# Three zero stores of fifteen rows issued from GpSimd in the last head group, and small stores at the end

## The chip, the cores and the metric

The kernel runs on one core of one Trainium2 chip. The metric is the device time of one execution in microseconds; smaller is better. Several executions of a kernel are timed, and the median is told. Beside the times there is a profile of one execution: for each engine what it ran and when, and for the DMA engines every packet that they moved.

The names used: TensorE (PE) multiplies matrices, VectorE (DVE) and ScalarE (ACT) work on rows of data, GpSimd (POOL) runs general operations and may issue transfers, SyncE (SP) issues transfers. Transfers between the device memory (DRAM) and the on-chip memory are carried out by 16 DMA engines that all issuers share.

## The reference: what is computed

The program is one decode step of a transformer block with its gradients. The block adds an attention over the last `W = 1024` of 4096 cached keys and a gated feed-forward network to its input. Outputs are the block's result and the gradients of its input, of both caches and of all weights.

```python
def _fwd_reference(A_x, A_k_cache, A_v_cache, A_wq, A_wo, B_x, B_w_gate, B_w_up, B_w_down):
    def _A_ref(x, k_cache, v_cache, wq, wo):
        ...
        W = min(4096, max(256, Sk // 4))
        k = jnp.repeat(k_cache[:, :, Sk - W:, :], rep, axis=1)
        v = jnp.repeat(v_cache[:, :, Sk - W:, :], rep, axis=1)
        scores = jnp.einsum("bhqd,bhkd->bhqk", q, k) * (Dh ** -0.5)
        p = _softmax(scores, axis=-1)
        ...
    def _B_ref(x, w_gate, w_up, w_down):
        return (_gelu(x @ w_gate) * (x @ w_up)) @ w_down
    x = A_x
    xn = _layernorm(x, axis=-1)
    return x + _A_ref(xn, A_k_cache, A_v_cache, A_wq, A_wo) + _B_ref(xn, B_w_gate, B_w_up, B_w_down)

def reference(...):
    _out, _vjp = jax.vjp(_f, A_x, A_k_cache, A_v_cache, A_wq, A_wo, B_w_gate, B_w_up, B_w_down)
    _grads = _vjp(grad_out)
    return (jnp.asarray(_out), *[jnp.asarray(_g) for _g in _grads])
```

The caches are `(4, 8, 4096, 128)` in bfloat16: 4 batches, 8 groups of heads, 4096 keys of 128 numbers. Their gradients have the same shape, and the first `K0 = 3072` keys of each of the 4 x 8 planes of each cache took no part in the attention. Their gradient is zero, but it has to be written: 64 planes (two caches) of 3072 keys x 128 numbers x 2 bytes = 768 KB each, 48 MB in all. That is the zero filling that the change is about.

## The kernel before: the parts concerned

Zeros lie in one on-chip tile of 128 rows x 6144 numbers (12288 bytes a row). One zero store writes one "region": two neighbouring planes of one cache gradient, 1.5 MB, as 128 pieces of 12288 bytes. There are 32 regions, and all are stored by SyncE's queue in turns with the other stores.

```python
    def store(eng, out, in_, kind):
        eng.nop()
        d = eng.dma_start(out=out, in_=in_)
        for k in ("rest", "zeros") if kind == "rest" else ("rest",):
            tc.declare_no_dep(d.ins, group=k, reason="stores write disjoint parts of the outputs")
        tc.add_to_no_dep_group(kind, d.ins)
        return d
    # ... (cut)
    ZR = 2
    ZW = K0 * Dh * ZR // P
    ztile = const.tile([P, ZW], BF16, name="ztile")
    zlist = deque((og, b, g) for b in range(B) for g in range(0, G, ZR) for og in (out_2, out_3))

    def zero(n=1):
        for _ in range(min(n, len(zlist))):
            og, b, g = zlist.popleft()
            store(nc.sync, og[b, g:g + ZR, 0:K0, :].rearrange("g (m j) d -> m g (j d)", m=P // ZR), ztile[:], "zeros")
    nc.gpsimd.memset(ztile[:], 0.0)
```

The attention runs over the 8 groups two at a time, in `NT = 4` turns. In each turn the scores and their gradients are made, then the pieces that write the gradients of values and keys (`dvdk`, staged in tiles `stg_dv` and `stg_dk`, three buffers) and of the weights (`dw`, tiles `osb_o` and `osb_q`). In the last turn four zero stores are put in at once; the rest of the list goes out at the end.

```python
        for t in range(NT):
            kv_steps(t, 0, 0)
            # ... (cut)
            softmax(t)
            kv_steps(t, 1, 1)
            if t == NT - 1:
                zero(4)
            link(len(chain))
            softmax_d(t)
            link()
            odq(t, 0)
            load_kv(t + 2, 1)
            # ... (cut)
            odT(t, 1)
            fin(t)
            if t + 2 < NT:
                load_w(t + 2)
            (k0, k1), (o0, o1, q0, q1) = dvdk(t, 1), dw(t)
            for p in (k0, o0, k1, o1, q0, q1):
                bg.extend(p)
        tick(len(bg))
        zero(len(zlist))

        fin_ps = []
        # ... (cut: the block's result and the gradient of its input,
        #      two stores of 4 KB from ScalarE's queue)
```

GpSimd issues six weight loads before this point (`load_w` for turns 1 to 3), each of 128 rows; all other transfers come from SyncE or ScalarE.

Of the kernel before, what the change touches and what calls it, by code (L numbers as in the profile page):

```python
# [18 lines left out]
def kernel(  # L19
# [28 lines left out]
    nc = tc.nc  # L48

    B, Sq, D = A_x.shape  # L50
    _, G, Sk, Dh = A_k_cache.shape
# [4 lines left out]
    K0 = Sk - W  # L56
# [4 lines left out]
    NT = G // GP  # L61
# [38 lines left out]
# [8 lines that stand above are left out]
# [12 lines left out]
    def load_w(t, eng=nc.gpsimd):  # L120
        pool = w_pool[t % 2]
        wo_t[t] = pool.tile([P, HG, D], BF16, name="wo_sb", tag="wo")
        eng.dma_start(out=wo_t[t][:], in_=wo_v[t])
        wq_t[t] = pool.tile([P, ND, CW], BF16, name="wq_sb", tag="wq")
        eng.dma_start(out=wq_t[t][:], in_=wq_v[t])

    def load_kv(t, k):
        if t >= NT:
            return
        d_, src, nm = ((k_t, A_k_cache, "kb"), (v_t, A_v_cache, "vb"))[k]  # L130
        for g in range(GP):
            tl = kv_pool[t % 2].tile([P, JB, Dh], BF16, name=nm, tag=nm)
            nc.sync.dma_start(out=tl[:].rearrange("p j d -> p (j d)"),
                              in_=src[:, t * GP + g, K0:Sk, :].rearrange("b (m j) d -> m b (j d)", j=JB))
            d_[(t, g)] = tl
# [22 lines left out]
# [4 lines that stand above are left out]
        for _ in range(min(n, len(zlist))):  # L162
            og, b, g = zlist.popleft()
            store(nc.sync, og[b, g:g + ZR, 0:K0, :].rearrange("g (m j) d -> m g (j d)", m=P // ZR), ztile[:], "zeros")


    nc.gpsimd.memset(ztile[:], 0.0)
    zero(3)
    ident_f = const.tile([P, P], FP32, name="ident_f")
    nc.vector.tensor_copy(out=ident_f[:], in_=ident[:])  # L170
# [91 lines left out]
    def tick(n):  # L262
        for _ in range(min(n, len(bg))):
            bg.popleft()()
# [3 lines left out]
    def link(n=1):  # L268
        for _ in range(min(n, len(chain))):
            chain.popleft()()  # L270
# [173 lines left out]
    def odq(t, k):  # L444
        pT, blks = st[t][("PT", "dST")[k]], (v_t, k_t)[k]
        cols = pT[:].rearrange("p j (y s) -> p j s y", s=SL)
        for j in range(JB):
            q, jj = j // JQ, j % JQ
            for g in range(GP):
                nc.tensor.matmul(od_ps[g * 32:g * 32 + B * rep, k, g, :], lhsT=cols[:, jj, g * NQ + q, :],  # L450
                                 rhs=blks[(t, g)][:, j, :], start=(j == 0), stop=(j == JB - 1),
                                 tile_position=(0, g * 32))
        rows = attw.tile([P, GP, Dh], BF16, name="od_r", tag=f"od_r{k}", bufs=2)
        if k == 0:
            nc.vector.tensor_copy(out=rows[:], in_=od_ps[:, k])  # L455
        else:
            nc.scalar.activation(out=rows[:], in_=od_ps[:, k], func=ACT.Copy, scale=scale)
        st[t][("o", "dq")[k]] = rows
        if k == 0:

            o_s = attw.tile([P, GP, rep, Dh], BF16, name="o_s", tag="o_s", bufs=2)
            for g in range(GP):
                nc.gpsimd.tensor_tensor(out=o_s[:, g], in0=rows[:, g].unsqueeze(1).broadcast_to([P, rep, Dh]),  # L463
                                        in1=msk_r[:].unsqueeze(2).broadcast_to([P, rep, Dh]), op=ALU.mult)
            st[t]["os"] = o_s

    def odT(t, k):
        rows = st[t][("o", "dq")[k]]
        T_ps = transposes([rows[:, g, :] for g in range(GP)], "odT")
        rT = attw.tile([P, GP, B, rep], BF16, name="od_T", tag=f"od_T{k}")  # L470
        for g in range(GP):
            nc.vector.tensor_copy(out=rT[:, g].rearrange("p b r -> p (b r)"), in_=T_ps[:, g, g * 32:g * 32 + B * rep])
        st[t][("oT", "dqT")[k]] = rT
# [206 lines left out]
    for f4 in range(NF4):  # L680
        held = {}
        n = min(4, NF - 4 * f4)
# [34 lines left out]
    with tc.tile_pool(name="kv_b", bufs=GP, reuse_waits="tile") as kv_b, \  # L717
            tc.tile_pool(name="w_b", bufs=1, reuse_waits="tile") as w_b, \
            tc.tile_pool(name="stage", bufs=3, reuse_waits="tile") as stage:
        kv_pool[1], w_pool[1] = kv_b, w_b  # L720
        zero()
        pre(0)
        load_w(1)
        load_kv(1, 0)
        for t in range(NT):
            kv_steps(t, 0, 0)
            if t == 0:
                zero()
                load_kv(1, 1)
                zero()  # L730
# [5 lines that stand above are left out]
            softmax_d(t)  # L736
            link()
            odq(t, 0)
            load_kv(t + 2, 1)
            if t + 1 < NT:  # L740
                pre(t + 1)
            link(len(chain))
            odT(t, 0)
            odq(t, 1)
            load_kv(t + 2, 0)
            tick(2)
# [6 lines that stand above are left out]
                bg.extend(p)  # L753
        tick(len(bg))
        zero(len(zlist))

        fin_ps = []
        for o in range(2):
            f_ps = ps_w.tile([B, ND, P], FP32, name="f_ps", tag="w")
            for c in range(ND):  # L760
                nc.tensor.transpose(f_ps[:, c, :], acc[:, o, c, :], ident_f[:])
            fin_ps.append(f_ps)
        acc_o = fin_ps[0][:].rearrange("b c p -> b (c p)")
        acc_d = attw.tile([B, P, ND], FP32, name="acc_d", tag="P_s")
        nc.vector.tensor_copy(out=acc_d[:].rearrange("b p c -> b c p"), in_=fin_ps[1][:])
        acc_d = acc_d[:].rearrange("b p c -> b (p c)")
        out_b = attw.tile([B, D], BF16, name="out_b", tag="pT")
        nc.vector.tensor_tensor(out=out_b[:], in0=acc_o, in1=x4[:], op=ALU.add)
        nc.scalar.dma_start(out=out_0.rearrange("b s d -> (b s) d"), in_=out_b[:])

        s1 = attw.tile([B, 1], FP32, name="s1", tag="m")
        nc.vector.reduce_sum(out=s1[:], in_=acc_d, axis=AX.X)
        pr = attw.tile([B, D], FP32, name="pr", tag="dS_s")
        s2 = attw.tile([B, 1], FP32, name="s2", tag="es")
        nc.vector.tensor_tensor_reduce(out=pr[:], in0=acc_d, in1=xn_f[:], scale=1.0, scalar=0.0,
                                       op0=ALU.mult, op1=ALU.add, accum_out=s2[:])
        nm1 = attw.tile([B, 1], FP32, name="nm1", tag="rr")
        nc.vector.tensor_scalar(out=nm1[:], in0=s1[:], scalar1=-1.0 / D, scalar2=None, op0=ALU.mult)
        nm2 = attw.tile([B, 1], FP32, name="nm2", tag="gs")
        nc.vector.tensor_scalar(out=nm2[:], in0=s2[:], scalar1=-1.0 / D, scalar2=None, op0=ALU.mult)  # L780
        nc.vector.scalar_tensor_tensor(out=pr[:], in0=xn_f[:], scalar=nm2[:, 0:1], in1=acc_d,
                                       op0=ALU.mult, op1=ALU.add)
        nc.vector.tensor_scalar(out=pr[:], in0=pr[:], scalar1=nm1[:, 0:1], scalar2=rstd[:, 0:1],
                                op0=ALU.add, op1=ALU.mult)
        dx_b = attw.tile([B, D], BF16, name="dx_b", tag="E_f")
        nc.vector.tensor_tensor(out=dx_b[:], in0=pr[:], in1=dy4[:], op=ALU.add)
        nc.scalar.dma_start(out=out_1.rearrange("b s d -> (b s) d"), in_=dx_b[:])
# [30 lines left out]
```

## Time and profile before

| what | value |
|---|---|
| time, median of 3 | 283.25 us (282.78 to 283.46) |
| span of the profiled execution | 281.0 us |
| PE, DVE, ACT, POOL busy | 72%, 58%, 42%, 14% |
| moved by the DMA engines | 112.12 MB, mean 399 GB/s |
| of it read and written in DRAM | 30.68 MB and 81.01 MB |
| SyncE's queue (q1), share of 16 DMA engines' time | 89.6% |
| GpSimd's queue (q0) | 5.6% |
| zero stores | 32, of 1536 KB, 18.1 us from issue to landing (median) |

In the profile the span is cut into 40 equal slices, with a digit for the busy share of each engine in tenths; the row DMA is the mean busy share of the 16 DMA engines, and the row below it is what they moved in GB/s. The chain is followed back from the last instruction of a compute engine or queue to what released it. A transfer has landed when each DMA engine that has a part in it has reported its part. The trace has the time of each of these reports, 16 for a transfer of 128 rows.

### The profile page before, as it was taken

The numbers are of one execution on the slowest core, as the hardware profiler recorded it, in microseconds if no ns is written. First come the engines' busy times: TensorE is split into PE (matmuls) and PEld (weight loads), VectorE is DVE, ScalarE is ACT, GpSimd is POOL, SyncE is SP. The second block draws the span as 40 slices with busy tenths as digits, with TensorE's granted clock in tenths as the row PEclk, the third lists the DMA queues.
The fourth block names the chain that finished last, engine by engine and source line by source line (L and its number), as shares of the span: only waits on it lengthen the run. The fifth ranks groups of instructions, "written<-read, shape, count | busy, mean of one in ns | idle before, by whom it ended". The sixth has DMA issues, their size and how long they took to land.

```text
span 281.0 us, 6867 instructions
## 1 busy us (share of the span) xinstructions
PE 203.1 (72%) x2972; PEld 138.8 (49%) x2972; DVE 164.1 (58%) x313; ACT 117.8 (42%) x219; POOL 40.1 (14%) x40
## 2 busy tenths in 40 slices
PE   0276699959789889998999299898999599390000
PEld 0265476735456665566775156677556484140000
DVE  7946646645776655577666067767677728386000
ACT  2030386635035418764448056443866038370000
POOL 8600000007002150002250000223000400000000
PEclk9999589986999999999999969999999979977555
DMA  7999999999999999999999999999999999999990
GB/s 264 393 375 431 431 426 417 425 419 424 369 395 424 422 420 420 426 415 422 419 417 411 412 424 423 431 383 398 385 368 415 387 432 410 425 429 422 398 422 30
DMA packets 19565, 112.12 MB, mean 399 GB/s; under 512 B 1664, under 2 KB 4496, under 8 KB 11088
## 3 DMA queue, kind: packets, MB, share of 16 engines
q1 hardware_dynamic: 17744, 103.56, 89.6%
q0 software_dynamic: 1632, 6.29, 5.6%
q10 hardware_dynamic: 160, 1.84, 1.9%
q8 instruction: 23, 0.38, 0.5%
q14 instruction: 6, 0.05, 0.0%
HBM read 30.68 MB, written 81.01 MB: 397 GB/s over the span
## 4 chain that ended last, share of the span: by engine, by line
PE 47%; DMA 22%; DVE 16%; ACT 4%; issue 2%; SPq 0%; DVEq 0%; ACTq 0%
DMA out_dram<-stg_dv 13%; PE T_ps L279 8%; PE kv_ps L484 7%; DMA wd_sb<-in_B_w_down_dram 6%; PE S_ps L345 5%; PE od_ps L450 5%; DMA out_dram<-osb_g 4%; DVE T_sb L98 3%; DVE dS_s L367 2%; PE wdT_ps L279 2%; PE dwq_ps L520 2%; PE acc_ps L256 2%; PE dwd_ps L660 2%; DVE P_s L367 2%; PE wgT_ps L279 2%
## 5 line engine op out<-in xcount | busy, mean ns | idle before, releaser
L98 DVE COPY T_sb<-T_ps 128x1024 bf16<-128x1024 bf16 x64 | 44.1, 688 | 26.7 <-PE T_ps L279 26.5
L97 ACT CAST stg_dk<-kv_ps 128x512 bf16<-128x512 f32 x52 | 29.2, 588 | 31.2 <-PE kv_ps L484 12.4
L97 ACT CAST stg_dv<-kv_ps 128x512 bf16<-128x512 f32 x51 | 28.1, 588 | 24.9 <-PE kv_ps L484 24.3
L484 PE MATMUL kv_ps<-qmr,dS_s 128*128 128x512 bf16 x64 | 23.9, 414 | 11.3 <-ACT stg_dk L97 10.6
L463 POOL TENSOR_TENSOR o_s<-od_r,msk_r 128x512 bf16<-128x512 bf16 x8 | 9.1, 1157 | 110.2 <-DVE od_r L455 80.9
L484 PE MATMUL kv_ps<-domr,P_s 128*128 128x512 bf16 x64 | 21.3, 382 | 0.0
L279 PE MATMUL T_ps<-ident,vb 128*128 128x128 bf16 x256 | 20.3, 225 | 0.4 <-DVE T_sb L98 0.4
L279 PE MATMUL T_ps<-ident,kb 128*128 128x128 bf16 x256 | 20.4, 225 | 0.0
L279 PEld LDWEIGHTS <-kb 128*128 128x128 bf16 x256 | 17.5, 101 | 4.5 <-issue 1.3
L279 PEld LDWEIGHTS <-vb 128*128 128x128 bf16 x256 | 17.2, 101 | 5.0 <-issue 3.2
L97 ACT CAST osb_q<-dwq_ps 128x512 bf16<-128x512 f32 x25 | 14.6, 587 | 8.3 <-PE dwq_ps L520 7.4
L329 POOL TENSOR_TENSOR domr<-r,msk 128x1024 bf16<-128x1024 bf16 x4 | 7.6, 1892 | 71.2 <-DVE r L326 65.1
L97 ACT CAST osb_g<-dwg_ps 128x512 bf16<-128x512 f32 (+1 forms) x25 | 12.3, 544 | 12.3 <-PE dwg_ps L673 6.3
L97 ACT CAST osb_o<-dwo_ps 128x512 bf16<-128x512 f32 x24 | 13.9, 586 | 4.5 <-PE dwo_ps L505 2.9
L98 DVE CAST stg_dk<-kv_ps 128x512 bf16<-128x512 f32 x12 | 8.0, 688 | 12.0 <-DMA out_dram<-stg_dv 11.2
L98 DVE COPY wgT<-wgT_ps 128x1024 bf16<-128x1024 bf16 x14 | 9.6, 686 | 6.8 <-PE wgT_ps L279 6.8
L345 PE MATMUL S_ps<-T_sb,qm 128*32 128x256 bf16 x128 | 12.7, 387 | 0.6 <-DVE T_sb L98 0.5
L345 PE MATMUL S_ps<-T_sb,dom 128*32 128x256 bf16 x128 | 12.7, 388 | 0.1
L505 PE MATMUL dwo_ps<-dyr,o_s 128*128 128x512 bf16 x32 | 12.4, 413 | 0.3 <-ACT stg_dk L97 0.2
L98 DVE COPY woT<-woT_ps 128x1024 bf16<-128x1024 bf16 x16 | 11.0, 686 | 2.7 <-PE woT_ps L279 2.3
L484 PEld LDWEIGHTS <-dS_s 128*128 128x128 bf16 x64 | 6.2, 101 | 12.2 <-issue 11.1
L520 PE MATMUL dwq_ps<-od_r,xnm 128*128 128x256 bf16 x64 | 11.6, 274 | 0.3 <-ACT osb_q L97 0.2
(188 smaller groups left out, 385.0 us busy)
## 6 DMA issues: line engine op xcount, KB each, us to landing
out_dram<-ztile SPq DMA_DIRECT2D x32, 1536.0 KB, 18.1
kb<-in_A_k_cache_dram SPq DMA_DIRECT2D x8, 1024.0 KB, 17.4
vb<-in_A_v_cache_dram SPq DMA_DIRECT2D x8, 1024.0 KB, 20.7
out_dram<-stg_dv SPq DMA_DIRECT2D x8, 1024.0 KB, 13.0
out_dram<-stg_dk SPq DMA_DIRECT2D x8, 1024.0 KB, 20.8
out_dram<-osb_o SPq DMA_DIRECT2D x8, 512.0 KB, 17.4
out_dram<-osb_q SPq DMA_DIRECT2D x8, 512.0 KB, 13.8
out_dram<-osb_g SPq DMA_DIRECT2D x8, 448.0 KB, 14.3
```

The source lines that it names most:

```text
L97: return nc.scalar.copy(out=out, in_=in_)
L98: return nc.vector.tensor_copy(out=out, in_=in_)
L256: nc.tensor.matmul(ps[:, c, :], lhsT=lf(c), rhs=rhs, start=(k == 0), stop=(k == len(terms) - 1))
L279: nc.tensor.transpose(ps[:, i, :], a, ident[:])
L329: nc.gpsimd.tensor_tensor(out=mr[:].rearrange("p g q d -> p (g q) d"), in0=r4[:, k, :].unsqueeze(1).broadcast_to([P, SL, Dh]), in1=msk[:]. ...
L345: nc.tensor.matmul(ps[b * RB:(b + 1) * RB, :], lhsT=zt[:, b * GP + g, c0:c0 + RB], rhs=T_sb[:].rearrange("p (x b) -> p b x", b=B)[:, b, :] ...
L367: nc.vector.scalar_tensor_tensor(out=out[:], in0=src[:].unsqueeze(2).broadcast_to([P, WQ, B]), scalar=rr[:, 0:1], in1=mskb[:].unsqueeze(1) ...
L450: nc.tensor.matmul(od_ps[g * 32:g * 32 + B * rep, k, g, :], lhsT=cols[:, jj, g * NQ + q, :], rhs=blks[(t, g)][:, j, :], start=(j == 0), st ...
L463: nc.gpsimd.tensor_tensor(out=o_s[:, g], in0=rows[:, g].unsqueeze(1).broadcast_to([P, rep, Dh]), in1=msk_r[:].unsqueeze(2).broadcast_to([P ...
L484: nc.tensor.matmul(mps[:].rearrange("p q d -> p (q d)"), lhsT=src[:, j * P:(j + 1) * P], rhs=mr[:, g].rearrange("p q d -> p (q d)"), start ...
L505: nc.tensor.matmul(mps[:], lhsT=o_s[:, g].rearrange("p r d -> p (r d)")[:, i:rep * Dh:rep], rhs=dyr[:], start=True, stop=True)
L520: nc.tensor.matmul(mps[:, i].rearrange("p g d -> p (g d)"), lhsT=xnm[:, i2 * 2 + i, c * P:(c + 1) * P], rhs=dq_r[:].rearrange("p g d -> p ...
```

## The change

The two last regions of the list (four planes) are no longer stored by SyncE at the end. In the last turn, after `odq(t, 0)`, GpSimd issues seven stores: for each of three planes one store of 15 rows, in which every row is written four times (15 x 4 x 12288 bytes, 2880 of the 3072 keys), and short stores of 5, 1, 1 and 12 rows before, between and after. The fourth plane, and the keys that the first two planes lack, are stored by SyncE at the end: one store of 64 rows x 12288 bytes, and four small ones of 12, 6, 8 and 5 rows.

The purpose is to give the 16 DMA engines unequal work. A store of 15 rows can be spread over 15 engines and leaves one out; [...]the rows add up to 5 + 15 + 1 + 15 + 1 + 15 + 12 = 64[...]. The number of bytes written stays as it is.

```diff
+    def zero_keys(eng, n, w, r=1):
+        og, b, g, k0 = zh
+        dst = og[b, g, k0:k0 + n * r * w, :].rearrange("(m r j) d -> m r (j d)", m=n, r=r)
+        src = ztile[0:(n - 1) * 9 + 1:9, 0:w * Dh] if n < 16 else ztile[0:n, 0:w * Dh]
+        if r > 1:
+            src = src.unsqueeze(1).broadcast_to([n, r, w * Dh])
+            store(eng, dst, src, "zeros")
+        else:
+            store(eng, dst[:, 0, :], src, "zeros")
+        zh[3] += n * r * w
+
+    def zero_15(first):
+        late = []
+        for og, b, g in (zlist.pop(), zlist.pop()):
+            for gg in (g, g + 1):
+                zh[:] = [og, b, gg, 0]
+                if len(late) == 3:
+                    late.append(list(zh))
+                    break
+                if not late:
+                    zero_keys(first, 5, 1)
+                zero_keys(first, 15, 48, 4)
+                if len(late) < 2:
+                    zero_keys(first, 1, (7, 16)[len(late)])
+                else:
+                    zero_keys(first, 12, 16)
+                    assert zh[3] == K0
+                late.append(list(zh))
+        return late
+
+    zh = []
@@ -736,6 +770,8 @@
             odq(t, 0)
+            if t == NT - 1:
+                late = zero_15(nc.gpsimd)
             load_kv(t + 2, 1)
@@ -753,6 +789,13 @@
         tick(len(bg))
         zero(len(zlist))
+        zh[:] = late[3]
+        zero_keys(nc.sync, 64, 48)
+        for i, (n0, w0, n1, w1) in enumerate(((12, 10, 6, 10), (8, 12, 5, 16))):
+            zh[:] = late[i]
+            zero_keys(nc.sync, n0, w0)
+            zero_keys(nc.sync, n1, w1)
+            assert zh[3] == K0
```

`zero_keys(eng, n, w, r)` stores `n` rows of `w` keys, each `r` times; blank lines are cut from the diff.

## The prediction

> **What bounds the kernel now.** I read the page's slices first, because the change moves transfers and no arithmetic.
>
> ```profile
> DMA  7999999999999999999999999999999999999990
> GB/s 264 393 375 431 431 426 417 425 419 424 369 395 424 422 420 420 426 415 422 419 417 411 412 424 423 431 383 398 385 368 415 387 432 410 425 429 422 398 422 30
> ```
>
> The DMA engines are at 9 tenths or more from the second slice to the one before the last, while PE is busy for 72% and no other engine for more. The kernel is bound by what 16 DMA engines move. But the last slice (274 to 281 us) holds 30 GB/s: 7 us, 2.5% of the span, in which nearly nothing is moved. So I asked for the end in stretches (after the times: busy time and count of PE, PEld, DVE, ACT, POOL; clock; DMA share; GB/s):
>
> ```profile
> 264.00:272.00 8.00, 0.00 (x0) 0.00 (x0) 0.00 (x0) 0.00 (x0) 0.00 (x0) 0.50 1.04 423
> 272.00:274.00 2.00, 0.00 (x0) 0.00 (x0) 0.00 (x0) 0.00 (x0) 0.00 (x0) 0.50 0.95 402
> 274.00:275.50 1.50, 0.00 (x0) 0.00 (x0) 0.00 (x0) 0.00 (x0) 0.00 (x0) 0.50 0.18 74
> 275.50:280.00 4.50, 0.00 (x0) 0.00 (x0) 0.00 (x0) 0.00 (x0) 0.00 (x0) 0.50 0.05 22
> ```
>
> No compute engine works there. The share falls from 0.95 to 0.05, which is about one engine of 16 (0.0625). The transfers of 275.5 to 280.5 us alone:
>
> ```profile
> DMA packets 10, 0.10 MB, mean 20 GB/s; under 512 B 2, under 2 KB 2, under 8 KB 2
> ```
>
> Eight of the ten packets are big ones, 12288 bytes each, and in the trace's packet records they start 0.457 us apart with no overlap: one DMA engine works off zeros alone. The completion reports agree. The last zero store (issued at 263.85) is reported by twelve engines at 274.38 to 274.65, by three at 274.85, 275.38 and 275.50, and by one at **279.94**. The same picture, one report 4 to 6 us behind the others, stands at every large store issued since 219 us: the store issued at 222.77 has fifteen reports up to 238.68 and one at 242.92. I call this one the late engine. It is late long before the end, and only at the end does that cost time.
>
> The chain of waits misleads here. Its last pieces are
>
> ```profile
> 256.64 0.54 DVE pr L783
> 257.21 0.68 DVE dx_b L786
> ```
>
> so it stops 22 us before the end, at the last arithmetic. What follows is in the issue rows of SyncE's queue,
>
> ```profile
> 259.52 1.72 SPq L103 DMA_DIRECT2D out_dram<-osb_q  x2
> 263.25 1.98 SPq L103 DMA_DIRECT2D out_dram<-ztile  x2
> ```
>
> and in its waits, where the last one of the program is a store of zeros (columns: total us, times, longest):
>
> ```profile
> SPq L813 <- DMA out_dram<-ztile: 7.2, 2, 3.6
> ```
>
> The end is therefore: landing of the late engine's last zeros (279.94) + 1.1 us of closing = 281.0.
>
> [...]The trace shows one slow engine; it doesn't number it. All I can tell: the two 4-row result stores (4 packets of 1024 bytes each, at 258.8 and 262.1 us) fit into the packet rows of four engines that are not the late one[...]. [...]with or without GpSimd's loads, the slices from the second to the one before the last hold 368 to 432 GB/s.
>
> **The change part by part.** A plane is 64 pieces of 12288 bytes, 4 for each of 16 engines.
>
> Removed at the end: two zero stores of 128 pieces, 16 pieces per engine, 16 x 0.457 = 7.3 us of each engine.
>
> Added at the end: one plane, 4 pieces per engine (1.8 us), and the small stores. [...]
>
> Added at about 224 us: POOL's last operations (the two `o_s` products, 3.0 us from 221.2) end at 224.3, and GpSimd waits for no transfer still under way. Its three 15-row stores have 60 pieces each, 12 per engine that has a part in all three, 5.5 us. GpSimd's loads came in packets of 4096 bytes at 159 ns in the records; if the zeros do too, it is 36 x 0.159 = 5.7 us.
>
> What each engine then does: an ordinary engine has -16 + 12 + 4 = 0 pieces plus its share of what was spread. If one engine is left out by all three stores, 12 pieces are spread over 15 others: 0.8 piece, 0.37 us on average, 0.46 at the worst. The late engine has 12 pieces less, 5.48 us, and some of the short ones back (0.1 to 0.8 us[...]). That 12 fits the lateness so well (279.94 - 274.48 = 5.46 us, 11.9 pieces) speaks for a change made with this engine in view.
>
> So if it is left out all three times: late engine 279.94 - 5.5 + 0.1 to 0.8 = 274.6 to 275.3. The twelve: 274.5 + 0.4 + 0.2 for small packets = 275.1. The three that are 0.4 to 1.1 us behind them become the last: 275.5 + 0.2 to 0.6 = about 275.9. Gain 279.94 - 275.9 = 4.0 us; time 283.25 - 4.0 = **279.25**.
>
> In between nothing else should move. GpSimd's packets push the twelve back by 5.5 us between 224 and about 245 us, that is to where the late engine already is. Buffers (`stg_dv`, 11.7 us of waiting from 233.6 us in the chain) come free at the last report, which was the late engine's anyway. The last arithmetic ends 22 us before the span does, so even 5 us more of it stay hidden.
>
> **The rivals.**
>
> 1. *Not the same engine, or not the late one, is left out.* For it: the short one-row stores are built as 16 pieces of 56 and 128 numbers, not as one row[...]. Hit once, the late engine loses 4 pieces, 1.8 us, less up to 0.5: about 281.7. Never hit, it keeps its 12 pieces and gets small packets on top: 283.25 + 0.2 to 0.6 = 283.6. [...]
> 2. *The staging buffers come later.* If the ordinary engines fall behind by more than the late one leads (5.5 us), `stg_dv` and `stg_dk` free later and SyncE's window, which waits for older transfers before each issue, opens later. A slip under 5 us costs nothing, as said; to cost time the rings would have to run dry before 264 us, which the full share of 1.04 at 264 to 272 speaks against. Worth 0 to 1 us.
> 3. *Small transfers.* SyncE issues six DMAs at the end instead of two, and each waits for an older landing. The last one waits for the zeros issued at 251.63, landed at 268.93 (late engine), with 5 us of queued work left then: hidden. If a late issue is left over it is 1 to 2 us after 275: 280 to 281.
> 4. *The lateness is made by GpSimd's transfers.* Then these stores would renew it even on an engine they leave out. The late report's distance to the next one grows from 1.3 to 4.2 us about 150 us, when the third pair of weight loads is moving, but is also built up at 175 to 209 with none. Cost up to 2 us.
>
> **Range and chances.** All three stores on the late engine: I give 0.6, at 278.8 to 279.9. Some of them, or something of rivals 3 and 4: 0.2, at 280 to 282. None: 0.2, at 283 to 284. The middle of this lies near 279.6; I say **279.7**, with 278.6 to 283.7 for 8 in 10. More than 2% (below 277.6) would need 5.7 us, more than the 5.46 us by which the late engine trails: 0.03. Slower than 288.9 has no mechanism here: 0.02. Within 2%: 0.95.
>
> **What would show it.** Right: the stretch with a share near 0.06 at the end shrinks from 4.5 us to under 1 us; the sixteen reports of the last large store lie within 1.5 us; GpSimd's queue has 2.2 MB more, in the slices from 224 us; the span ends near 277. Wrong: a late engine still alone after 276 us, with a trail of 12288-byte packets 0.457 us apart (rival 1; its length tells how many stores hit); a share under 0.9 before 270 (rival 2); short packets last (rival 3); or a late report that trails by 2 us or more in spite of 12 pieces less (rival 4).

## The result

The changed kernel takes **290.43 us** (289.82 to 290.92), the kernel before 283.12 us beside it: ratio 1.0257, 95% interval 1.0233 to 1.0281. It is slower by 7.3 us. I had said 279.7 us, in a range that ended at 283.7, and had given a slowdown by over 2% a chance of 0.02.

### The profile page after: what moved, and what is told of

The parts are those of the page before. It is cut to its first block, busy times and chain, and to the rows that moved or that the text cites. A ratio compares the mean times of both kernels' runs of the same rounds, so it can differ in the third digit from the quotient of the medians.

```text
span 288.6 us, 6868 instructions
## 1 busy us (share of the span) xinstructions
PE 202.6 (70%) x2962; PEld 139.5 (48%) x2972; DVE 164.2 (57%) x313; ACT 117.6 (41%) x219; POOL 44.0 (15%) x47
## 4 chain that ended last, share of the span: by engine, by line
DMA 44%; PE 32%; DVE 10%; ACT 4%; issue 2%; SPq 0%; DVEq 0%; ACTq 0%
DMA out_dram<-stg_dv 23%; DMA out_dram<-osb_o 9%; PE T_ps L313 6%; DMA wd_sb<-in_B_w_down_dram 5%; PE kv_ps L518 4%; PE S_ps L379 4%; PE od_ps L484 4%; DMA out_dram<-osb_g 4%; DMA out_dram<-osb_d 3%; PE dwq_ps L554 2%; DVE T_sb L98 2%; PE wdT_ps L313 2%; PE acc_ps L290 1%; DVE P_s L401 1%; PE dwo_ps L539 1%
## 5 line engine op out<-in xcount | busy, mean ns | idle before, releaser
L518 PE MATMUL kv_ps<-qmr,dS_s 128*128 128x512 bf16 x62 | 23.0, 406 | 19.6 <-ACT stg_dk L97 18.9
L518 PE MATMUL kv_ps<-domr,P_s 128*128 128x512 bf16 x58 | 19.5, 379 | 0.1
```

The source lines that it names most:

```text
L518: nc.tensor.matmul(mps[:].rearrange("p q d -> p (q d)"), lhsT=src[:, j * P:(j + 1) * P], rhs=mr[:, g].rearrange("p q d -> p (q d)"), start ...
```

## The profile after

The slices of the changed kernel's page, 7.2 us each:

```profile
DMA  7999999999999999999999999999999999999960
GB/s 263 396 383 424 439 413 429 424 417 390 370 416 418 414 425 422 424 426 421 409 407 420 422 428 420 404 407 385 408 386 384 390 361 355 410 426 418 400 162 25
```

The DMA row looks as before: 9 nearly everywhere. The row below it doesn't. There are two dents that the kernel before lacks: 361 and 355 GB/s in slices 33 and 34 (231 to 245 us), and 162 in slice 39 (274 to 281 us). The engines are busy there and move less. The end in stretches, with the columns that the prediction gave (the last two are DMA share and GB/s):

```profile
272.00:274.00 2.00, 0.00 (x0) 0.00 (x0) 0.00 (x0) 0.00 (x0) 0.00 (x0) 0.50 1.04 378
274.00:275.50 1.50, 0.00 (x0) 0.00 (x0) 0.00 (x0) 0.00 (x0) 0.00 (x0) 0.50 1.23 289
275.50:280.00 4.50, 0.00 (x0) 0.00 (x0) 0.00 (x0) 0.00 (x0) 0.00 (x0) 0.50 0.67 149
280.00:284.00 4.00, 0.00 (x0) 0.00 (x0) 0.00 (x0) 0.00 (x0) 0.00 (x0) 0.50 0.17 56
284.00:288.00 4.00, 0.00 (x0) 0.00 (x0) 0.00 (x0) 0.00 (x0) 0.00 (x0) 0.50 0.04 16
```

From 275.5 to 280 us two thirds of the engines' time are in use for 149 GB/s. At a share of 0.67 the engines moved 0.67 / 0.95 x 402 = 283 GB/s before: the packets take twice as long. Then, from 284 us, one engine is alone again: the lone late engine has not gone. The GpSimd phase is the stretch from 225 to 245 us, in which GpSimd's new stores run. First the kernel before, then the changed one:

```profile
225.00:235.00 10.00, 9.94 (x174) 7.69 (x171) 4.44 (x10) 4.66 (x9) 0.00 (x0) 0.83 0.99 414
235.00:245.00 10.00, 5.85 (x22) 1.94 (x20) 5.16 (x9) 5.45 (x10) 0.00 (x0) 1.00 1.01 421
```

```profile
225.00:235.00 10.00, 9.77 (x172) 7.66 (x170) 4.45 (x10) 4.80 (x10) 2.89 (x6) 0.87 1.01 372
235.00:245.00 10.00, 5.60 (x21) 1.84 (x19) 5.15 (x8) 5.27 (x10) 0.00 (x0) 0.98 0.99 356
```

The share is the same, the rate is 10% and 15% lower. The chain has the wait for `stg_dv` at 19.4 us, where it was 11.7. First before, then after:

```profile
233.63 11.70 DMA out_dram<-stg_dv
```

```profile
233.38 19.39 DMA out_dram<-stg_dv
```

```profile
265.25 0.68 DVE dx_b L829
```

but its end, the last arithmetic at 265.9 us, is still 21 us ahead of the last landing (287.15).

From the reports of completion I followed the late engine through both traces:

| report of the late engine | before | after | later by |
|---|---|---|---|
| zeros issued at 222.8 / 222.7 us | 242.92 | 250.27 | 7.35 |
| zeros issued at 237.8 / 238.2 | 255.39 | 262.82 | 7.43 |
| zeros issued at 251.6 / 259.1 | 268.93 | 279.15 | 10.22 |
| the last store | 279.94 | 287.15 | 7.21 |

It was to stay free of GpSimd's 12 pieces. Its reports slip by 7.35 us instead, more than 12 pieces take at the old pace (12 x 0.457 = 5.5 us). Then it lost another 2.8 us before 279.15 us. The work that was taken from the end gave it back 3.0 us, where 12 pieces are worth 5.5.

## The experiments

Five theories stood beside each other: **A**, the rows from which the zeros are read slow the packets, in the GpSimd phase and in the 64-row store at the end; **B**, only the GpSimd phase matters; **C**, stores from GpSimd as such are slow; **D**, the late engine isn't left out because the one-row stores don't move the start (the engine on which the next GpSimd store begins; that it moves at all is an assumption); **E**, the start is another one. By what means rows could slow a packet the traces don't show; what the runs can show is whether the rows matter.

### The plane at the end from all 128 rows

```diff
-        zero_keys(nc.sync, 64, 48)
+        zero_keys(nc.sync, 128, 24)
```

> The changed kernel, but the plane that SyncE stores at the end is read from all 128 rows of the zero tile (128 x 6144 bytes) instead of from rows 0 to 63 (64 x 12288 bytes). Theory A (reading many pieces from few neighbouring rows [...]slows packets, 460 ns to as much as 1858 ns for 12288 bytes after 273 us): the packets of that plane come down to about 0.23 us each, the engines other than the late one end within 2 to 4 us of each other instead of 7.5, and the time falls by 2.5 to 4 us, to 286.5 to 288. Rival B (all of the loss is in the GpSimd phase, and the end only waits for the late engine): 290 within 0.7.

Measured: 286.81 us, ratio 1.0106 (1.0081 to 1.0132). That is 3.6 us under the changed kernel.

```profile
270.00:275.00 5.00, 0.00 (x0) 0.00 (x0) 0.00 (x0) 0.00 (x0) 0.00 (x0) 0.50 1.00 393
275.00:280.00 5.00, 0.00 (x0) 0.00 (x0) 0.00 (x0) 0.00 (x0) 0.00 (x0) 0.50 0.46 182
```

182 GB/s at a share of 0.46 is 396 at full share: the usual pace. In the packet records the median of SyncE's 12288-byte packets from 274 us on is 885 ns in the changed kernel (longest 1858); here the five that start after that have 466 ns, and the plane's own packets of 6144 bytes have 234 ns, as expected. The edit halves the pieces as well as it changes the rows, but the length isn't what was slow: stores of 128 rows have the same 12288-byte pieces, at 462 ns in the median before. The engines other than the late one still end their parts of this plane 5.0 us apart (275.21 to 280.26), more than theory A said; that spread comes in from the GpSimd phase, where the zeros issued at 238.3 us already show it (255.60 to 260.70). Half of the loss is this one line, and B has fallen.

### As many bytes from GpSimd, evenly

Shown against the changed kernel; the few-row stores at the end are left out too.

```diff
-                zero_keys(first, 15, 48, 4)      # and the short stores
+                zero_keys(first, 128, 24)        # three planes
...
+        zero_keys(nc.sync, 128, 24)              # the fourth, at the end
```

> As many bytes from GpSimd at the same place, but evenly: three planes as stores of 128 rows x 24 keys on all 16 engines, no short stores, and the fourth plane from SyncE at the end in the same shape. No engine is left out. Theory A (the source rows, not the issuer, cost the time): packets keep their usual length and the time is that of the kernel before, 283.2 within 0.8. Rival C (stores from GpSimd as such slow the DMA engines, or delay the staging buffers): 286 or more, with a DMA rate below 400 GB/s between 225 and 245 us.

Measured: 283.70 us, ratio 1.0012 (0.9997 to 1.0027).

```profile
225.00:235.00 10.00, 9.75 (x172) 7.71 (x174) 4.45 (x12) 4.66 (x9) 1.14 (x3) 0.83 1.00 409
235.00:245.00 10.00, 6.12 (x25) 2.07 (x23) 5.33 (x9) 5.44 (x10) 0.00 (x0) 1.00 1.02 419
```

The rate is the old one. GpSimd as the issuer costs nothing that can be measured, and the late engine neither gains nor loses (it trails by 4.2 us at the end). C has fallen, and so has the prediction's fourth rival, for an even split.

### The 15 rows next to each other

```diff
-        src = ztile[0:(n - 1) * 9 + 1:9, 0:w * Dh] if n < 16 else ztile[0:n, 0:w * Dh]
+        src = ztile[0:15, 0:w * Dh] if n == 15 else ...      # the others as they were
```

> The changed kernel with the 15-row stores read from rows 0 to 14 of the zero tile, next to each other, instead of from every ninth row. Theory A: [...]the GpSimd phase gets longer, other packets are slowed too, and the time grows by 3 to 10 us, to 293 to 300. Rivals B and C (source rows don't matter): 290.4 within 0.7.

Measured: 300.11 us, ratio 1.0579 (1.0533 to 1.0624).

```profile
225.00:235.00 10.00, 9.77 (x172) 7.52 (x169) 4.63 (x11) 5.04 (x10) 2.79 (x6) 0.89 1.04 298
235.00:245.00 10.00, 5.38 (x19) 1.75 (x18) 4.96 (x8) 5.04 (x10) 0.00 (x0) 0.96 1.04 202
245.00:255.00 10.00, 0.00 (x0) 0.00 (x0) 0.00 (x0) 0.00 (x0) 0.00 (x0) 0.50 0.99 213
```

All DMA engines are busy (share 0.96 to 1.04), and from 235 us on half the data moves (202 GB/s, against 421 in the kernel before). GpSimd's 12288-byte packets between 226 and 248 us have a mean of 1702 ns, against 545 in the changed kernel. Only the place of the rows differs between the two.

### Other short stores between

```diff
-                    zero_keys(first, 1, (7, 16)[len(late)])
+                    zero_keys(first, 9, 1)
+                    zero_keys(first, 8, 1)
```

with the end store of 128 rows, and the small stores at the end fitted to the keys that are left.

> As e1_end_128rows, but each one-row short store (built as 16 pieces, so perhaps spread over all engines and moving nothing) is replaced by stores of 9 and 8 rows of one key, 17 rows, which move the start by one if short stores move it by their rows. Theory D (the late engine isn't left out because the one-row stores move nothing): all three 15-row stores now leave out the same engine. If that is the late one, it loses 12 pieces, its lone tail is gone, and the time is 5 us or so under e1's, 281 to 283. Rival E (the start isn't where the change takes it to be): the same engine is left out three times, but another one, and the time is e1's within 1 us or longer by up to 1.

Measured: 286.62 us, ratio 1.0110 (1.0074 to 1.0146), the same as without it (286.81). The late engine took its 12 pieces again: its report of the zeros issued at 223.2 us comes at 250.84. So the one-row stores aren't why the late engine is hit; E, or no movement at all, is left.

### A probe: on which engines does a GpSimd store run?

Everything is left out of this kernel but sixteen steps. In each, SyncE keeps eight engines busy with a store of 8 rows, and GpSimd issues one store beside it.

```diff
+    for i, (n, w, r) in enumerate(first + then):     # rows, keys, repeats
+        nc.vector.memset(ztile[:, 0:6144], 0.0)      # waits for the step before
+        put(nc.sync, of3, 16384 * (i % 2), 8, 48, 16)
+        put(nc.gpsimd, of2, 16384 * (i % 2), n, w, r)
```

> A probe that leaves the whole computation out: sixteen steps one after another, in each a SyncE store of 8 rows (16 pieces of 12288 bytes a row, so eight DMA engines are kept busy for about 7.4 us alone) and beside it one GpSimd store: 5 rows, 15x4, one row of 7 keys, 15x4, one row of 16 keys, 15x4, 12 rows (the change's order), then 15x4, 9, 8, 15x4, 9, 8, 15x4, 15x4, 4 rows. The packet records tell how many engines a GpSimd store uses and how many of them are among the eight busy ones. If short stores move the start by their rows: 15 engines with 4 pieces each; the one left out is the same for all 15-row stores of the first seven if a one-row store uses one engine (theory: rotation as the change means it), and goes down by one each time if it uses all sixteen (theory D). If the start doesn't move at all, the 15-row stores use the same 15 engines whatever lies between.

Measured, from the packet records (pieces of GpSimd's store on the eight busy engines and on the other eight):

```
GpSimd store            steps                   on the busy eight   on the others
5 rows                  1                               5                 0
15 rows x 4             2, 4, 6, 8, 11, 14, 15         32                28     (each of the seven)
one row, 16 pieces      3                               8                 8
one row, 16 pieces      5                               9                 7
12 rows                 7                               8                 4
9 rows                  9, 12                           8                 1
8 rows                  10, 13                          8                 0
4 rows                  16                              3                 1
```

The counts of steps 5 and 16 are off by one; where tiny packets pass between two engines my assignment can slip. The reports of completion bear out the 15-row stores without any counting. All seven have the same pattern: one report early (the engine with no piece), seven 1.6 to 1.9 us later, and eight, those of the busy engines, another 1.6 to 2.4 us after these. In step 2 these are 24.04, 25.63 to 25.83 and 28.23 to 28.31 us. The engine left out is thus never among the busy eight, and if the start moved by the rows, 8 rows after 9 could not all be there again. **None of these stores moved the start.** As far as the counts tell, GpSimd's 8 rows run on the eight engines of SyncE's 8 rows (8 of 8 pieces, twice), 9 rows on these and one more (8 and 1, twice), 12 rows on these and four more (8 and 4, once), and the engine left out by 15 rows is in all seven one that a store of 8 rows doesn't use. The engines have no numbers in the traces; below, number n is the one that a store of n + 1 rows uses and a store of n rows doesn't. The next experiment finds the late engine to be number 4 by this count, with a part in the store of 8 rows, so it is never the one left out.

### Rows 32, 36, 40 and so on

The next edit reads every fourth row from row 32 on. That these rows suit the engines better was a guess beforehand: no trace here shows which engine reads which rows. In the expectation "engines 0 to 14" stands for a start that doesn't move.

```diff
-        src = ztile[0:(n - 1) * 9 + 1:9, 0:w * Dh] if n < 16 else ztile[0:n, 0:w * Dh]
+        src = ztile[32:32 + (n - 1) * 4 + 1:4, 0:w * Dh] if n < 16 else ztile[0:n, 0:w * Dh]
...
-((12, 10, 6, 10), (8, 12, 5, 16))
+((12, 10, 6, 10), (8, 12, 4, 20))
```

again with the end store of 128 rows.

> As e1_end_128rows, but the rows of the short and the 15-row stores are read from rows 32, 36, 40 and so on of the zero tile[...]; and the last small store has 4 rows of 20 keys in place of 5 of 16. Theory A with rows on engines 0 to 14: no packet is slowed, and the 3.1 us by which e1 is over e2 vanish or turn into a gain: 281 to 284. Theory A with rows on other engines: still slowed, 285.5 to 288. Marker: the late engine's report is missing from the 4-row store and present in the 5-, 6- and 8-row ones if it is engine number 4.

Measured: 284.27 us, ratio 1.0032 (1.0022 to 1.0042), 2.5 us under the same kernel with every ninth row and 0.3 us above the range expected. Up to 0.2 us of this may be the last small store, in which the late engine has no part any more (an estimate: its reports of the small stores come 0.19 us apart). The mean of GpSimd's big packets falls from 550 to 486 ns, the rate between 225 and 245 us rises from 378 and 356 to

```profile
225.00:235.00 10.00, 9.13 (x161) 7.31 (x163) 4.88 (x12) 4.64 (x9) 3.85 (x8) 0.83 1.01 407
235.00:245.00 10.00, 6.45 (x38) 2.40 (x36) 5.46 (x10) 5.45 (x10) 0.00 (x0) 1.00 1.00 400
```

The marker spoke too. In this run the reports of the stores of 12, 6 and 8 rows each have a lone late one (281.83, 282.02, 282.21), the 4-row store's lie between 277.83 and 277.90. In the changed kernel the 5-row store had its late one (287.15, the one before it at 282.64). So the late engine has a part in five rows and none in four: it is number 4. What is left over the even version, some 0.6 to 0.8 us, has no experiment of its own.

### Sixteen rows, from row 32 and from row 36

As the even version, against which the edits are shown, but each plane from 16 rows, written four times; once from rows 32, 36, ... 92, once shifted by four rows.

```diff
+        src = ztile[32:32 + (n - 1) * 4 + 1:4, 0:w * Dh] if n == 16 else ...   # e7
+        src = ztile[36:36 + (n - 1) * 4 + 1:4, 0:w * Dh] if n == 16 else ...   # e8
...
-                    zero_keys(first, 128, 24)
+                    zero_keys(first, 16, 48, 4)
```

> As e2_even_from_gpsimd, but each plane from GpSimd is one store of 16 rows, each written four times (64 pieces of 12288 bytes, all 16 engines), read from rows 32, 36, ... 92[...]. Theory A (only the part of the tile matters, not that one row is read four times): e2's time, 283.7 within 0.8. Rival F (reading one row repeatedly, or few rows, is what slows): 286 or more.

> As e7_16rows_own, but from rows 36, 40, ... 96[...]. Theory A: packets of both queues are slowed from 460 to 500 to 900 ns in the GpSimd phase, and the time is 2 to 4 us over e7's. Rival F: as e7 within 0.7.

Measured: 283.44 us, ratio 1.0002 (0.9989 to 1.0014) from row 32; 286.80 us, ratio 1.0112 (1.0073 to 1.0150) from row 36. The rates, first from row 32, then from row 36:

```profile
225.00:235.00 10.00, 9.77 (x173) 7.70 (x170) 4.45 (x10) 4.78 (x10) 0.64 (x2) 0.87 1.00 413
235.00:245.00 10.00, 5.64 (x21) 1.84 (x19) 5.15 (x8) 5.31 (x10) 0.00 (x0) 0.98 1.03 428
```

```profile
225.00:235.00 10.00, 9.88 (x173) 7.75 (x173) 4.37 (x10) 4.66 (x9) 0.80 (x2) 0.83 1.00 363
235.00:245.00 10.00, 5.92 (x22) 1.98 (x21) 5.23 (x9) 5.44 (x10) 0.00 (x0) 1.00 0.99 341
```

The two kernels differ by the first row alone, 32 or 36. Same pieces, same bytes, same places written: 3.4 us. The mean of GpSimd's packets is 472 and 603 ns, and that of SyncE's beside them 469 and 531. Rival F (reading one row often) is out, and the rows are shown to be the cause. How they act was not shown.

### Relieving engine 4 in a way that works

With the late engine in five rows and not in four, a store of four rows can spare it. This goes back to the kernel before and changes its last two regions only, from SyncE.

```diff
-        zero(len(zlist))
+        zero(len(zlist) - 1)
+        og, b, g = zlist.pop()
+        zero_keys(og, b, g, 0, 16, 4)                # 4 pieces an engine
+        k0 = 0
+        for n, r in ((16, 1), (4, 12)):              # f3: (16, 1), (5, 9), (3, 1)
+            k0 = zero_keys(og, b, g + 1, k0, n, r)
```

All rows are read from 32, 36, 40 and so on.

> The kernel before, with the last two regions stored by SyncE so that the DMA engines get unequal shares: one region as before (8 pieces of 12288 bytes an engine), one plane from 16 rows (4 each), 16 pieces from 16 rows (1 each), and 48 pieces from 4 rows (12 each, read from rows 32, 36, 40, 44). If a store of 4 rows runs on engines 0 to 3 and the late engine is number 4, the late engine has 13 pieces instead of 16: it ends 3 x 0.457 = 1.4 us earlier, engines 0 to 3 have 25 and end at about the same time, and the time is 281.9 within 0.5 (ratio 0.995). If the late engine is one of 0 to 3 it ends 9 pieces later: 287. If it is another one from 5 to 15: 281.9 as well, and f3 tells.

> As f1_four_rows, but the 48 pieces come from 5 rows (9 each, 45) and 3 rows (1 each). If the late engine is number 4, it is now among those that get more: 22 pieces instead of 16, 6 x 0.457 = 2.7 us later than before, 286.0 within 0.6. If it is one of 5 to 15, it has 13 pieces and the time is f1's within 0.6.

Measured: **282.21 us, ratio 0.9949 (0.9930 to 0.9968)** with four rows; 286.15 us, ratio 1.0091 (1.0073 to 1.0109) with five. One row more puts the late engine among those that get extra pieces, and costs 3.9 us. The end of the four-row kernel:

```profile
274.00:275.50 1.50, 0.00 (x0) 0.00 (x0) 0.00 (x0) 0.00 (x0) 0.00 (x0) 0.50 0.29 123
275.50:280.00 4.50, 0.00 (x0) 0.00 (x0) 0.00 (x0) 0.00 (x0) 0.00 (x0) 0.50 0.22 96
```

A share of 0.22 to 0.29 is some four engines of 16, where one was alone before. With five rows one is alone again:

```profile
278.00:283.00 5.00, 0.00 (x0) 0.00 (x0) 0.00 (x0) 0.00 (x0) 0.00 (x0) 0.50 0.06 25
```

In the four-row kernel four reports of the 4-row store come at 279.03 to 279.29, the late engine's last one at 279.42: five engines end together. It is the only version here that beats both kernels.

## Why the prediction was wrong

- **What bounds the kernel, and the lone late engine:** right. The four packets of each result store fitted four other engines, and a 4-row store at the end has no part on this one either (in the run with rows from 32 on its reports lie between 277.83 and 277.90 us, the late engine's between 281.83 and 282.21). It trails by 5.5 us, and its time can be moved: three pieces less were worth 1.05 us of the 1.4 that 0.457 us a piece gives (282.21 against 283.26), with engines 0 to 3 now ending beside it.
- **"If one engine is left out by all three stores" and it is the late one (0.6):** this step failed. In seven of seven 15-row stores of the probe the engine left out was one that an 8-row store doesn't use, whatever short stores lay between; the late engine is one that a 5-row store does use. It kept its 12 pieces, and the 4.0 us of gain didn't come. My first rival had the outcome ("never hit"), with one-row stores as the reason; the run with 9 and 8 rows shows that this was not the reason (286.62 us, against 286.81 with one-row stores). I had assumed a moving start, with the trace silent, and then let the sum of 64 rows (four times 16) and the fit of the 12 pieces speak for it. They show only what the change was meant to do. What fits the probe for stores of 4 to 15 rows is one row per engine, on the same engines whatever was stored before (in the counts above, off by one in two steps).
- **"12 per engine ..., 5.5 us", at 0.457 us a piece:** the second failure. I carried the length of a packet over to packets read from other rows. Measured means between 226 and 248 us: 545 ns for GpSimd's, 532 for SyncE's beside them (468 before). The medians are 471 and 474 (462 before): a part of the packets is hit, up to 1419 ns. In time 286.81 - 283.70 = 3.1 us, of which changing the rows alone took back 2.5; the other 0.6 us stay unexplained.
- **"Added at the end: one plane, 4 pieces per engine (1.8 us)":** the third failure, of the same kind. From rows 0 to 63 the pieces took 885 ns in the median, and slowed what the late engine still had to do. In time 290.43 - 286.81 = 3.6 us. Together 6.7 of the 7.3 us. The rest, 283.70 - 283.12 = 0.6 us, is half a slightly slower kernel before in that comparison (283.44) and half a difference (0.26 us) whose interval includes zero.
- **The buffers (second rival):** right that it costs nothing. The wait for `stg_dv` grew by 7.7 us and the last arithmetic came 8.0 us later, and it stayed 21 us ahead of the end.
- **Small transfers (third rival):** the last small store was issued at 279.16, not 268.93, since the landing it waits for slipped by 10.2 us. Its other engines had reported by 282.64; only the late one was awaited (287.15), and that for its older work.
- **Lateness by GpSimd's transfers (fourth rival):** not seen; the even version has no more of it.
- **Packets of 4096 bytes for the zeros:** not so, and harmless; GpSimd's packets were 12288 bytes.
- **The chances:** 0.02 for slower by over 2% said that no mechanism was there. None of the rivals asked from which rows the new stores read, though the diff shows two new choices of rows (every ninth, and 0 to 63).

## What to carry to other kernels

In this kernel, which the transfers bound, a new store had three sides: how many bytes, on which engines, and from which rows of the on-chip memory. Here it paid to read rows 32, 36, 40 and so on: 284.27 us against 286.81 with every ninth row, and 283.44 against 286.80 with rows 36, 40 and so on. Compare GB/s with the DMA share: in these runs a full share at a lower rate came with the rows read (421 GB/s before, 356 with every ninth row, 202 with rows 0 to 14). A lone engine at the end is worth looking for, but find out its number with a marker (a store of n rows and one of n + 1) before work is steered around it: here 282.21 us with four rows, 286.15 with five.

## What the runs showed that I had not expected

- The same bytes on the same engines cost 3.4 us more when the rows are shifted by four (283.44 and 286.80), and 15 neighbouring rows bring the rate down to 202 GB/s at a full share.
- In seven of seven steps a GpSimd store of 15 rows left out an engine that a SyncE store of 8 rows doesn't use, and 8 rows from GpSimd ran on the same eight engines as SyncE's (8 of 8 pieces, twice): no moving set.
- Why engine 4 trails was not tried. The last report's distance to the one before it is 0.8 us for the zeros issued at 110 us, 1.9 at 141, 3.8 at 194, and 4.1 to 4.6 from 223 us on. As far as the last report is the same engine's throughout, this engine keeps pace with the others from there on. Nor was it tried why, with rows 32, 36 and so on, the engine that 15 rows leave out didn't run ahead by its 12 pieces.
